# A chunked state-space scan feeding a squared-ReLU network: chunks of 64 tokens instead of 128, and every small product as a 32x32 tile

## The chip, the cores and the metric

The kernel runs on one core of a Trainium2 chip. The metric is the device time of one execution in microseconds (us), lower is better. The times of before are three runs on a chip; the profile is one more execution of the same program.

## What is computed

Inputs: x (4 batches, 8 heads, 768 tokens, 32 features), decays a (one per batch, head and token), B and C (16 states), and two matrices w_in (256 x 2048) and w_out (2048 x 256). Cut to what matters, the reference is:

```
for each chunk of tokens:                       # any chunk length gives the same y
    cum = cumsum(log a)                         # within the chunk
    M[i,j]   = (C_i . B_j) * exp(cum_i - cum_j)  for j <= i, else 0
    y        = M @ x  +  exp(cum_i) * (C_i @ state)
    state    = exp(cum_last) * state + sum_j exp(cum_last - cum_j) * B_j x_j
out = square(relu(y @ w_in)) @ w_out            # over 3072 tokens, the 8 heads' y side by side
```

The recurrence is per batch and head; the state is 16 x 32. The feed-forward part is most of the arithmetic.

## The kernel before, in words

**Units.** The 3072 tokens are cut into 12 units of 256 tokens (`UNITS`: three pieces j of a batch's 768 tokens, four batches b; units 0 to 3 are j=0, 4 to 7 j=1, 8 to 11 j=2). A token is 2p+r, with p the partition and r in 0, 1. Before, a unit has two chunks i of 128 tokens (64 partitions each).

**Scan of a unit k.** The decays become cumulative products P (`scan`, `prep_p`), C is multiplied by P (`prep_c`), x by 1/P (`prep_x`), B is copied as it is (`prep_b`). C and B of all heads stand side by side in a tile `jt`, which is transposed to `bct`: for units 0 to 3 by six products on TensorE (PE) and two copies (`ph_tr`, `ph_trc`), from unit 4 on by a DMA transpose. Then come the small products, all on PE:

- `ph_mt` (L213): scores C.B of the unit, 16 products of 32 x 64 weights on 256 columns, into all of banks 0 to 3. VectorE (DVE) multiplies them by the causal mask (`ph_mask`, L222, four of 512 elements) into `mts`.
- `ph_u` (L238): what each chunk adds to the state, 16 products of 64 x 32 on 64 columns (8 for j=2, whose last chunk has no successor).
- `ph_carry` (L238): C times the state before a chunk, 4 products of 128 x 128 on 128 columns (2 for j=0). Its weights `Sd` hold the state in a block-diagonal form that GpSimd (POOL) builds with `Pquad` (`ph_sd`, L329).
- `ph_intra` (L238): mts times x, 32 products of 64 x 32 on 128 columns, added in PSUM to the carry.
- `ph_t`, `ph_uc`: ScalarE (ACT) copies y to `T` and the state sums to `us`. `ph_z` (L313, L318, DVE) runs the recurrence over the chunks.

**Feed-forward.** For block k and each of eight groups: `mm1` (L388) is four products of 128 x 128 on 256 columns from T and w_in into one bank, ACT takes relu (L393), DVE squares (L399), `mm2` (L413) is four products of 128 x 128 on 256 columns into the block's accumulation bank. So there are 12 x 8 x 2 = 192 groups of four.

**Order.** All engines run their instructions in the order in which they are issued, and that order is the hand-written string `ORDER`: `c3` is `mm1` of block 2, group 3; `C3` its `mm2`; `mt1`, `mk1` (masks), `tr2`, `pc2`, `pb2`, `px2`, `ld3` (load of unit 3 on SP's queue) act on a unit; `rg6` is one region: carry of unit 5, u of unit 6, intra of unit 5, scores of unit 6, on PE one after the other. Units 1 and 2 are done in pieces (`eu`, `ey`, `et`) between the first groups. `bank()` hands out PSUM banks in turn from the list `turn` (4 and 5 first, then 4, 5, 0, 1, then 4, 5, 6) for mm1 and for y and u in `region`.

**Opening.** L439 on: loads of a, then C, B, x of units 0 and 1 on SP and ACT; a cumulative product; unit 0 up to T[0]; products of ones (`idle_products`, L458) fill PE while it has nothing to do, 21 in all. Weights come on POOL's queue, which converts them to bf16: w_in in two halves (groups 0 to 3, groups 4 to 7), w_out in four quarters. The first half is issued after a copy (`gate_w`) that waits for unit 0's B, the second after a copy (`gate_b`) that waits for unit 2's B; unit 3's load waits behind a POOL memset (`gate`).

Of the kernel before, what the change touches and what calls it, by code (L numbers as in the profile page):

```python
# [13 lines left out]
ALU = mybir.AluOpType  # L14
# [16 lines left out]
def kernel(  # L31
# [17 lines left out]
        a0 mt1 mk1 a1 sc1 a2 ld2 mk1 mk1 a3 A0 ms1 eu1 A1 sd1 A2 ey1 A3 iv0 la et1 b0 b1 b2 b3 w1 w2 px2 sn B0 ld3 pc2  # L49
        B1 w3 pb2 ld4 a4 tr2 B2 tc2 a5 b4 mt2 pc3 B3 mk2 p2 A4 mk2 b5 mk2 mk2 a6 eu2 pb4 sd2 pb3 B4 b6 A5 tr3 px3 tc3  # L50
        pc4 ey2 b7 a7 iv1 et2 B5 B6 A6 rg3 c0 px4 za3 sa3 ld5 tr4 mk3 mk3 c1 bk0 c2 zb3 A7 sb3 c3 mk3 pq pc5 px5 c4
        mk3 B7 ld6 c5 bk1 C0 c6 rg4 zb0 sb0 pb5 C1 mk4 C2 mk4 za4 c7 C3 tr5 ld7 zb1 zb4 sa4 sb4 pb6 d0 mk4 C4 C5 d1
        sb1 d2 mk4 C6 pc6 C7 d3 px6 d4 D0 rg5 tr6 mk5 za5 zb5 sa5 sb5 D1 iv2 mk5 d5 D2 pb7 d6 d7 D3 zb2 e0 mk5 e1 sb2
        D4 mk5 D5 ld8 pc7 e2 D6 e3 px7 D7 rg6 e4 za6 sa6 tr7 zb6 mk6 e5 sb6 e6 e7 mk6 E0 E1 E2 E3 ld9 px8 mk6 f0 E4 f1
        pc8 E5 pb8 E6 mk6 f2 f3 E7 rg7 mk7 F0 f4 za7 tr8 F1 F2 f5 f6 f7 g0 zb7 sa7 sb7 mk7 F3 mk7 F4 pc9 pb9 px9 ld10
        g1 F5 mk7 g2 F6 g3 F7 rg8 za8 zb8 sa8 sb8 g4 G0 mk8 tr9 g5 G1 mk8 g6 G2 g7 G3 mk8 h0 G4 pc10 pb10 px10 ld11 h1
        G5 mk8 h2 G6 h3 G7 rg9 za9 zb9 sa9 sb9 h4 H0 mk9 tr10 h5 H1 mk9 h6 H2 h7 H3 mk9 i0 H4 pc11 pb11 px11 i1 H5 mk9
        i2 H6 i3 H7 rg10 za10 zb10 sa10 sb10 i4 I0 mk10 tr11 i5 I1 mk10 i6 I2 i7 I3 mk10 j0 I4 j1 I5 mk10 j2 I6 j3 I7
        rg11 za11 zb11 sa11 sb11 j4 J0 mk11 j5 J1 mk11 j6 J2 j7 J3 mk11 k0 J4 k1 J5 mk11 k2 J6 k3 J7 rg12 k4 K0 k5 K1
        k6 K2 k7 K3 l0 K4 l1 K5 l2 K6 l3 K7 l4 L0 l5 L1 l6 L2 l7 L3"""  # L60
    WIN = [(0, 4), (4, 8)]
    WOUT = [(0, 2), (2, 4), (4, 6), (6, 8)]
# [8 lines left out]
    fpool = ctx.enter_context(tc.tile_pool(name="fpool", bufs=4))  # L71
    hpool = ctx.enter_context(tc.tile_pool(name="hpool", bufs=8))
# [3 lines left out]
    UNITS = [(b, j) for j in range(3) for b in range(4)]  # L76

    eye_f = const.tile([128, 128], FP32, name="eye_f")
    eye_b = const.tile([128, 128], BF16, name="eye_b")
    mask = const.tile([128, 512], BF16, name="mask")  # L80
    tri = const.tile([128, 2, 128], BF16, name="tri")
    warm = const.tile([128, 2], BF16, name="warm")
    quad = const.tile([128, 4], FP32, name="quad")
# [4 lines left out]
    a_nat = [const.tile([n, 128], FP32, name=f"a_nat{n}") for n in (64, 128)]  # L88
    a_cl = [const.tile([n, 128], FP32, name=f"a_cl{n}") for n in (64, 128)]
    cp = [const.tile([n, 128], FP32, name=f"cp{n}") for n in (64, 128)]  # L90
    pick_p = [const.tile([n, m], FP32, name=f"pick_p{n}") for n, m in ((64, 8), (128, 16))]
    P_sb = const.tile([128, 2, 96], FP32, name="P_sb")
    Pinv = const.tile([128, 2, 96], FP32, name="Pinv")
    Ptot = const.tile([128, 24], FP32, name="Ptot")
    Pquad = const.tile([128, 24, 4], FP32, name="Pquad")
    jt = [const.tile([128, 2, 3, 128], BF16, name=f"jt{i}") for i in range(3)]
    w_in_b = [wpool.tile([128, 2, (f1 - f0) * 256], BF16, name=f"w_in_b{i}") for i, (f0, f1) in enumerate(WIN)]
# [4 lines left out]
    def total(i, b, j):  # L102
        return 4 * i + b if j == 0 else 8 + 8 * i + 4 * (j - 1) + b

    def load_a(j, u, eng):
        row = 32 * u if j == 0 else 64 * u + 32 * (j - 1)
        t = a_nat[j > 0]
        eng.dma_start(out=t[row:row + 32, :], in_=_dap(a, j * 256 + u * 128, [[S, 32], [1, 128]]))
# [13 lines left out]
    def gate(k, what):  # L122
        b, j = UNITS[k]
        w = {"B": N, "C": N, "x": D}[what]
        t = nat.tile([128, NH, 2 * w], FP32, tag=f"{what}_nat", name=f"{what}_nat{k}")
        loaded.setdefault(k, {})[what] = t
        nc.gpsimd.memset(t[:, 0, 0:1], 0.0)

    def load_w_in(i):
        f0, f1 = WIN[i]  # L130
        n = (f1 - f0) * 256
        nc.gpsimd.dma_start(out=w_in_b[i], in_=_dap(moe_w_in, f0 * 256, [[2048, 128], [128 * 2048, 2], [1, n]]))

    def load_w_out(i):
        f0, _ = WOUT[i]
# [3 lines left out]
    def group_of(groups, fp):  # L139
        i = next(i for i, (f0, f1) in enumerate(groups) if f0 <= fp < f1)  # L140
        return i, fp - groups[i][0]

    live = {}

    def prep_c(k, eng, P=None):
        b, j = UNITS[k]
        for g in range(2):
            p = P_sb if P is None else P
            st = 96 if P is None else 32
            col = (j * 32 if P is None else 0) + b * 8 + 4 * g  # L150
            eng.tensor_tensor(  # L151
                out=_fap(jt[k % 3], 128 + 144 * g, [[384, 2], [32, 4], [1, 16]]),
                in0=_fap(loaded[k]["C"], 128 * g, [[16, 2], [32, 4], [1, 16]]),
                in1=_fap(p, col, [[st, 2], [1, 4], [0, 16]]), op=ALU.mult)

    def prep_b(k, eng, gs=(0, 1)):
        for g in gs:
            o = _fap(jt[k % 3], 16 * g, [[384, 2], [32, 4], [1, 16]])
            i = _fap(loaded[k]["B"], 128 * g, [[16, 2], [32, 4], [1, 16]])
            if eng is nc.scalar:  # L160
                eng.copy(out=o, in_=i)
            else:
                eng.tensor_copy(out=o, in_=i)  # L163

    def prep_x(k, eng):
# [8 lines left out]
        live.setdefault(k, {})["xs"] = xs  # L174

    def ph_tr(k, banks):

        v = live.setdefault(k, {})
        bct = big.tile([128, 2, 3, 128], BF16, tag="bct", name=f"bct{k}")
        v["bct"] = bct  # L180
        if banks is None:
            nc.sync.dma_start_transpose(out=bct.rearrange("p r w t -> p (r w) t"),
                                        in_=jt[k % 3].rearrange("p r w t -> p (r w t)"))
            return
        v["tr"] = []
        for r in range(2):
            h = banks[r]
            o = 0 if banks[0] != banks[1] else r * 192
            tr = pp[:, h, o:o + 192].bitcast(BF16)
            for w in range(3):  # L190
                nc.tensor.transpose(tr[:, w * 128:(w + 1) * 128], jt[k % 3][:, r, w, :], eye_b)  # L191
            v["tr"].append(tr)

    def ph_trc(k, engs):
        v = live[k]
        for r, eng in enumerate(engs):
            if eng is None:
                continue
# [6 lines left out]
    T = {}  # L205

    def ph_mt(k):
        v = live[k]
        bct = v["bct"]
        for r in range(2):  # L210
            for u in range(2):
                for q in range(4):
                    nc.tensor.matmul(  # L213
                        pp[64 * u:64 * u + 64, q, r * 256:r * 256 + 256],
                        bct[32 * q:32 * q + 32, r, 0, u * 64:u * 64 + 64],
                        _fap(bct[32 * q:32 * q + 32], 128 + u * 64, [[128, 2], [384, 2], [1, 64]]),
                        start=True, stop=True, skip_group_check=True,
                        tile_position=(32 * q, 64 * u))
        v["mts"] = big.tile([128, 4, 2, 2, 128], BF16, tag="mts", name=f"mts{k}")

    def ph_mask(k, q):
        nc.vector.tensor_tensor(out=live[k]["mts"][:, q].rearrange("p r g i -> p (r g i)"),  # L222
                                in0=pp[:, q, :], in1=mask, op=ALU.mult)

    def ph_score(k, q):
        sc = big.tile([128, 512], BF16, tag="sc", name=f"sc{k}_{q}")
        nc.scalar.copy(out=sc, in_=pp[:, q, :])  # L227
        live[k].setdefault("sc", {})[q] = sc

    def ph_mask_sb(k, q, eng):  # L230
        eng.tensor_tensor(out=live[k]["mts"][:, q].rearrange("p r g i -> p (r g i)"),  # L231
                          in0=live[k]["sc"][q], in1=mask, op=ALU.mult)

    def mm(begun, i, quads, dst, w, v, pos):
        need = [(i, q) for q in quads if (i, q) not in begun]
        begun.update(need)
        assert len(need) in (0, len(quads))
        nc.tensor.matmul(dst, w, v, start=bool(need), stop=False, skip_group_check=True,  # L238
                         **({} if pos is None else {"tile_position": pos}))

    def ph_carry(k, h, begun):
        for i in range(2):
            S_i = live[k]["S"][i]
            if S_i is None:
                continue
            for g in range(2):
                mm(begun, i, range(4), pp[:, h[i], g * 128:(g + 1) * 128], S_i[:, g * 128:(g + 1) * 128],
# [52 lines left out]
    def ph_z(k, i):  # L300
        b, j = UNITS[k]
        v = live[k]
        if j == 2 and i == 1:
            return
# [396 lines left out]
```

## Time and profile before

| what | us |
|---|---|
| median of three runs | 121.46 |
| the runs | 121.38, 121.46, 122.57 |
| profiled execution, first to last instruction (its span) | 119.2 |
| first mm1 starts | 12.5 |
| last mm2 product starts | 115.5 |
| PE busy from 40.35 to 102.85 | 62.50 of 62.50 |

The profile keeps no time of its own execution beyond the span: 121.46 - 119.2 = 2.3 us lie around it in the median run. Everything is read against that span. PE busy means that some product was in flight; the starts of neighbouring products tell how fast they go. From 40.35 us on PE never waits, until the last few products; the other engines have room there: DVE 51.49, ACT 44.13, POOL 27.57 of 62.50 us.

### The profile page before, as it was taken

The numbers are of one execution on the slowest core, as the hardware profiler recorded it, in microseconds if no ns is written. First come the engines' busy times: TensorE is split into PE (matmuls) and PEld (weight loads), VectorE is DVE, ScalarE is ACT, GpSimd is POOL, SyncE is SP. The second block draws the span as 40 slices with busy tenths as digits, with TensorE's granted clock in tenths as the row PEclk, the third lists the DMA queues.
The fourth block names the chain that finished last, engine by engine and source line by source line (L and its number), as shares of the span: only waits on it lengthen the run. The fifth ranks groups of instructions, "written<-read, shape, count | busy, mean of one in ns | idle before, by whom it ended". The sixth has DMA issues, their size and how long they took to land.

```text
span 119.2 us, 3961 instructions
## 1 busy us (share of the span) xinstructions
PE 111.2 (93%) x1609; PEld 93.1 (78%) x1609; DVE 83.0 (70%) x187; ACT 77.1 (65%) x158; POOL 49.3 (41%) x104
## 2 busy tenths in 40 slices
PE   7999879499989999999999999999999999999980
PEld 2533557278859898998998989989989889899960
DVE  5536593649489997999986798939848578445420
ACT  0735646475669667769565887686686777876840
POOL 7573387202676779565912297409120020000000
PEclk9999999999999999999999999999999999999999
DMA  2999968998991778998972854834023020020202
GB/s 41 198 157 162 219 139 97 185 178 162 192 144 59 188 149 149 198 135 178 74 150 93 139 108 138 145 105 105 3 89 70 0 96 0 0 93 0 88 0 88
DMA packets 47186, 13.46 MB, mean 113 GB/s; under 512 B 44288, under 2 KB 44736, under 8 KB 47168
## 3 DMA queue, kind: packets, MB, share of 16 engines
q1 hardware_dynamic: 44416, 10.83, 47.6%
q0 software_dynamic: 1120, 2.10, 11.0%
q10 hardware_dynamic: 1632, 0.28, 1.3%
q8 instruction: 12, 0.20, 0.7%
q14 instruction: 6, 0.05, 0.2%
HBM read 10.58 MB, written 3.15 MB: 115 GB/s over the span
## 4 chain that ended last, share of the span: by engine, by line
PE 83%; DMA 6%; ACT 3%; POOL 2%; DVE 1%; issue 1%; ACTq 0%; DVEq 0%
PE pp L388 33%; PE pp L413 32%; PE pp L238 6%; DMA w_in_b<-in_moe_w_in_dram 6%; PE pp L458 5%; PE pp L213 4%; ACT hb L393 2%; PE pp L191 1%; POOL mts L231 1%; PE pp L431 1%; POOL jt L151 1%; DVE mts L231 1%; PE pp L504 0%; ACT bct L201 0%; ACT sc L227 0%
## 5 line engine op out<-in xcount | busy, mean ns | idle before, releaser
L393 ACT ACTIVATE hb<-pp 128x512 bf16<-128x512 f32 x96 | 55.3, 599 | 25.5 <-PE pp L388 23.3
L388 PE MATMUL pp<-T,w_in_b 128*128 128x256 bf16 x384 | 54.8, 273 | 2.5 <-DMA w_in_b<-in_moe_w_in_dram 1.9
L399 DVE TENSOR_TENSOR h<-hb 128x512 bf16<-128x512 bf16 x96 | 45.2, 481 | 14.4 <-ACT hb L393 14.1
L413 PE MATMUL pp<-w_out_b,h 128*128 128x256 bf16 x384 | 54.9, 273 | 0.0
L388 PEld LDWEIGHTS <-w_in_b 128*128 128x128 bf16 x384 | 41.3, 114 | 6.0 <-DMA w_in_b<-in_moe_w_in_dram 2.3
L413 PEld LDWEIGHTS <-h 128*128 128x128 bf16 x384 | 36.7, 98 | 4.8 <-issue 0.8
L222 DVE TENSOR_TENSOR mts<-pp,mask 128x512 bf16<-128x512 f32 x44 | 29.4, 680 | 4.6 <-PE pp L213 4.6
L329 POOL TENSOR_TENSOR Sd<-z,Pquad 128x256 bf16<-128x256 f32 x16 | 10.7, 671 | 30.8 <-DVE z L313 24.3
L170 POOL TENSOR_TENSOR xs<-x_nat,Pinv 128x256 bf16<-128x256 f32 (+1 forms) x20 | 15.7, 798 | 3.3 <-DMA x_nat<-in_x_dram 1.8
L151 POOL TENSOR_TENSOR jt<-C_nat,P_sb 128x128 bf16<-128x128 f32 x22 | 9.7, 459 | 6.4 <-DMA C_nat<-in_C_dram 6.4
L458 PE MATMUL pp<-const-bfloat16-1.0 128*128 128x512 bf16 x13 | 6.2, 603 | 0.8 <-PEq L685 0.8
L420 ACT COPY osb<-pp 128x512 f32<-128x512 f32 x11 | 6.4, 586 | 0.2 <-PE pp L413 0.2
L313 DVE SCALAR_TENSOR_TENSOR z<-z,Ptot,us 128x64 f32<-128x64 f32 x8 | 2.2, 281 | 5.5 <-ACT us L297 5.4
L213 PE MATMUL pp<-bct 32*64 32x256 bf16 x192 | 5.3, 291 | 0.4 <-ACT us L294 0.3
L238 PE MATMUL pp<-mts,xs 64*32 64x128 bf16 x384 | 5.6, 219 | 0.0
L163 POOL CAST jt<-B_nat 128x128 bf16<-128x128 f32 x16 | 4.6, 317 | 1.9 <-DMA B_nat<-in_B_dram 1.9
L283 ACT CAST T<-pp 128x512 bf16<-128x512 f32 x8 | 4.7, 587 | 0.8 <-PE pp L238 0.5
L458 PEld LDWEIGHTS <-const-bfloat16-1.0 128*128 128x128 bf16 x21 | 2.1, 123 | 3.7 <-issue 3.4
L238 PE MATMUL pp<-bct,Sd 128*128 128x128 bf16 x40 | 4.2, 219 | 0.0
L238 PEld LDWEIGHTS <-xs 64*32 64x32 bf16 x384 | 3.8, 90 | 0.5
L238 PEld LDWEIGHTS <-jt 64*32 64x32 bf16 x160 | 1.6, 90 | 3.0 <-issue 1.0
L213 PEld LDWEIGHTS <-bct 32*64 32x64 bf16 x192 | 2.1, 105 | 2.1 <-issue 1.5
(71 smaller groups left out, 55.7 us busy)
## 6 DMA issues: line engine op xcount, KB each, us to landing
x_nat<-in_x_dram SPq DMA_DIRECT2D x11, 256.0 KB, 4.4
out_dram<-osb SPq DMA_DIRECT2D x11, 256.0 KB, 3.2
C_nat<-in_C_dram SPq DMA_DIRECT2D x11, 128.0 KB, 4.2
B_nat<-in_B_dram SPq DMA_DIRECT2D x11, 128.0 KB, 4.1
w_in_b<-in_moe_w_in_dram POOLq DMA_DIRECT2D x2, 512.0 KB, 7.1
w_out_b<-in_moe_w_out_dram POOLq DMA_DIRECT2D x4, 256.0 KB, 7.7
out_dram<-osl SPq DMA_DIRECT2D x2, 128.0 KB, 1.7
x_nat<-in_x_dram SPq DMA_DIRECT2D x1, 128.0 KB, 3.7
```

The source lines that it names most:

```text
L151: eng.tensor_tensor(out=_fap(jt[k % 3], 128 + 144 * g, [[384, 2], [32, 4], [1, 16]]), in0=_fap(loaded[k]["C"], 128 * g, [[16, 2], [32, 4], ...
L170: eng.tensor_tensor(out=_fap(xs, 256 * r, [[256, 2 // n], [32, 8], [1, 32]]), in0=_fap(loaded[k]["x"], 32 * r, [[32, 2 // n], [64, 8], [1, ...
L213: nc.tensor.matmul(pp[64 * u:64 * u + 64, q, r * 256:r * 256 + 256], bct[32 * q:32 * q + 32, r, 0, u * 64:u * 64 + 64], _fap(bct[32 * q:32 ...
L222: nc.vector.tensor_tensor(out=live[k]["mts"][:, q].rearrange("p r g i -> p (r g i)"), in0=pp[:, q, :], in1=mask, op=ALU.mult)
L238: nc.tensor.matmul(dst, w, v, start=bool(need), stop=False, skip_group_check=True, **({} if pos is None else {"tile_position": pos}))
L329: nc.gpsimd.tensor_tensor(out=_fap(S_d, 0, [[128, 2], [32, 4], [1, 32]]), in0=_fap(z, 0, [[32, 2], [0, 4], [1, 32]]), in1=_fap(Pquad, 4 * ...
L388: nc.tensor.matmul(pp[:, h, i * 256:(i + 1) * 256], _fap(w, g * w.shape[2] + (o // 2) * 512 + 2 * (o % 2) + i, [[4, 128]]), T[blk][:, g].r ...
L393: nc.scalar.activation(out=hb.rearrange("p i t -> p (i t)"), in_=pp[:, h, :], func=AF.Relu)
L399: nc.vector.tensor_tensor(out=h2, in0=hb, in1=hb, op=ALU.mult)
L413: nc.tensor.matmul(acc(blk, r), h2[:, i, r * 128:(r + 1) * 128], w_out_b[gi][:, 2 * o + i, :], start=first, stop=(fp == 7 and i == 1), ski ...
L420: nc.scalar.copy(out=osb, in_=pp[:, 6 if blk == 1 else 7, :])
L458: nc.tensor.matmul(pp[:, h, 0:cols], ones_b[:, 0:128], ones_b[:, 0:cols] if dep is None else dep, start=True, stop=True, skip_group_check= ...
```

## The change

- A unit has four chunks u of 64 tokens (32 partitions each), three of which have a successor at j=2.
- All small products are 32 x 32 tiles. Scores: 32 on 128 columns into columns 0 to 255 of banks 0 to 3. u: 32 on 64 columns (24 for j=2) into columns 384 to 447. Intra: 64 on 64 columns into columns 256 to 383 of the same banks. Carry: 32 on 64 columns (24 for j=0) into two banks of its own from `bank()`, one per half of the heads; the state needs no block-diagonal form any more (`Pquad` and `quad` go).
- Carry and intra no longer meet in PSUM: ACT copies the carry to `cs` and DVE adds the intra part into T (`ph_t`); for units 0 to 2 ACT copies intra (`ph_ys`) and DVE adds the carry (`ph_add`). The masks of a unit are two DVE instructions of 512 elements, not four; the recurrence is three or four z steps per unit, in place.
- Opening: a is loaded by one DMA per j on SP (128 rows of 64); scans run over 64 columns; prep_x of unit 0 moves from POOL to DVE; 15 products of ones remain, five of 128 columns and two of 256 among them. Unit 2 is loaded with unit 1.
- Weights come in eight pieces of two groups each, w_in and w_out in turn; the first is gated by unit 1's C. The gates of w_in's second half and of unit 3 go.
- `ORDER` is new: blocks a and b run their groups in twos, with banks 4 and 5 alone until block b ends, then 4, 5, 6. From `rg5` on the order is one region, then mm1 and mm2 alternating, as before.

The core of the diff; removed lines are left out.

```
+        a0 mA1 a1 u1 mB1 z1 sd1 A0 y1 A1 cy1 w6 pc2 b0 b1 w7 pb2 a2 B0 a3 B1 iv0 b2 b3 tr2 tc2 A2 mt2 A3 mA2 B2 mB2 px2
+        B3 la a4 a5 b4 b5 ld3 A4 u2 A5 z2 sd2 B4 B5 y2 a6 a7 sn sp cy2 b6 b7 pc3 pb3 px3 tr3 tc3 A6 A7 ld4 B6 c0 B7 c1
+        rg3 C0 c2 z3 sd3 iv1 pc4 pb4 C1 c3 mA3 px4 tr4 C2 c4 mB3 C3 c5 ld5 c6 pc5 pb5 px5 C4 c7 rg4 C5 z4 sd4 tr5 C6 mA4 d0 C7 d1 mB4 iv2 ld6 d2 pc6 pb6 px6 d3
+        rg5 d4 D0 z5 sd5 tr6 d5 D1 mA5 d6 D2 d7 mB5 D3 ld7 e0 D4 pc7 pb7 px7 e1 D5 e2 D6 e3 D7
...
+    PAIRS = [(0, 2), (2, 4), (4, 6), (6, 8)]
...
+    def load_a(j, eng):
+        eng.dma_start(out=a_nat[:, j, :], in_=_dap(a, j * 256, [[64, 4], [S, 32], [1, 64]]))
...
     def ph_mt(k):
...
         for r in range(2):
+            for u in range(4):
+                for R in range(4):
+                    p = slice(32 * R, 32 * R + 32)
                     nc.tensor.matmul(
+                        pp[32 * u:32 * u + 32, R, r * 128:r * 128 + 128],
+                        bct[p, r, 0, u * 32:u * 32 + 32],
+                        _fap(bct[p], 128 + u * 32, [[128, 2], [384, 2], [1, 32]]),
+                        start=True, stop=True, skip_group_check=True, tile_position=(32 * R, 32 * u))
...
+    def ph_carry(k, banks):
...
+        for s in range(4):
+            for R in range(4):
+                u = (R + s) % 4
+                if u == 0 and j == 0:
+                    continue
+                St = live[k - 4]["S"][:, 3] if u == 0 else live[k]["S"][:, u - 1]
+                p = slice(32 * R, 32 * R + 32)
+                for e in range(2):
+                    q = 2 * (R % 2) + e
+                    nc.tensor.matmul(pp[32 * q:32 * q + 32, banks[R // 2], u * 64:u * 64 + 64], St[p, e * 32:e * 32 + 32],
+                                     _fap(bct[p], 128 + 128 * e + 32 * u, [[384, 2], [1, 32]]), start=True, stop=True,
+                                     skip_group_check=True, tile_position=(32 * R, 32 * q))
...
+    def ph_u(k, base, begun):
...
+            for half in range(2):
+                for u in range(chunks(k)):
+                    p = slice(32 * u, 32 * u + 32)
+                    for R in ((0, 1), (2, 3))[(u + half) % 2]:
+                        mm(begun, u, R, pp[32 * R:32 * R + 32, base + u, U:U + 64],
+                           jt[k % 3][p, r, 0, 32 * R:32 * R + 32], v["xs"][p, r, 64 * R:64 * R + 64],
+                           (32 * u, 32 * R))
...
+    def ph_intra(k, base, begun):
         v = live[k]
         for g in range(2):
             for r in range(2):
+                for u in range(4):
+                    p = slice(32 * u, 32 * u + 32)
+                    for q in range(4):
+                        h = 4 * g + q
+                        mm(begun, u, q, pp[32 * q:32 * q + 32, base + u, Y + g * 64:Y + g * 64 + 64],
+                           v["xs"][p, r, 32 * h:32 * h + 32], v["mts"][p, h // 2, r, h % 2, :], (32 * u, 32 * q))
...
+    def region(y, u=None):
+
+        begun = set()
         h = sorted((bank(), bank()))
+        ph_carry(y, h)
         if u is not None:
+            ph_u(u, 0, begun)
+        ph_intra(y, 0, begun)
         if u is not None:
+            ph_mt(u)
+        ph_t(y, h)
+        if u is not None:
+            ph_us(u, 0)
...
+        gate = const.tile([128, 1], FP32, name="gate")
+        nc.gpsimd.tensor_copy(out=gate, in_=loaded[1]["C"][:, 0, 0:1])
+        load_w(0)
+        load_w(1)
+        idle_products(3, 5, 128, jt[0][:, 0, 0])
+        ph_mt(0)
...
+        ph_intra(0, 4, set())
+        ph_ys(0, 4)
+        ph_tr(1, (2, 3))
+        ph_carry(0, (0, 1))
+        ph_add(0, (0, 1))
         inv(8, 16)
...
+        load_w(3)
+        load_w(4)
+        load_w(5)
+        ph_mt(1)
...
         def second_p():
             h = bank()
+            for j in (1, 2):
+                prep_p(j, h, 64 * (j - 1))
...
+        def early_c(k):
+            h = sorted((bank(), bank()))
+            ph_carry(k, h)
+            ph_add(k, h)
```

In the new `ORDER`, `mA`, `mB` are the two masks of a unit, `u`, `y`, `cy` are u, intra and carry of units 1 and 2 (`early_c` above), `w6`, `w7` weight pieces, `la` the loads of a for j=1 and 2, `sn` and `sp` their scan and P (`second_p`); `rg3` is u and scores of unit 3 alone.

More of the change, by code (lines that the diff above doesn't have):

```diff
@@ L48 @@
     ORDER = """
[L49 to L53, printed above, removed]
@@ L219, in ph_mt @@
[L219 to L232, printed above, removed]
```

518 lines of the change are left out of this document (187 added, 331 removed).

## Prediction, made before the change was run

> **What bounds the kernel now.** I read the page's busy rows, then the chain that ended last in order of time, then the waits, then the timeline of PE alone around one region.
>
> ```profile
> span 119.2 us, 3961 instructions
> PE 111.2 (93%) x1609; PEld 93.1 (78%) x1609; DVE 83.0 (70%) x187; ACT 77.1 (65%) x158; POOL 49.3 (41%) x104
> ...
> PE   7999879499989999999999999999999999999980
> ```
>
> PE is the bound, except in the first third. The chain says the same: group after group of 0.44 us, and the region between them (238 and 213 are the small products).
>
> ```profile
> 46.13 0.44 PE pp L413 x4
> 46.57 0.73 PE pp L238 x52
> 47.30 0.35 PE pp L213 x16
> 47.65 0.54 PE pp L413 x4
> ```
>
> So every ns of small products in a region lengthens the kernel; masks and copies on DVE and ACT are hidden there. What a small product costs is seen in PE's timeline (start, us until the last of the group ends, what):
>
> ```profile
> 46.41 0.39 PE L238 MATMUL pp<-bct,Sd 128*128 128x128 bf16 x4
> 46.72 0.25 PE L238 MATMUL pp<-xs,jt 64*32 64x64 bf16 x16
> 46.79 0.51 PE L238 MATMUL pp<-mts,xs 64*32 64x128 bf16 x32
> 47.23 0.42 PE L213 MATMUL pp<-bct 32*64 32x256 bf16 x16
> 47.59 0.50 PE L413 MATMUL pp<-w_out_b,h 128*128 128x256 bf16 x3
> ```
>
> ```profile
> 103.00 0.42 PE L238 MATMUL pp<-mts,xs 64*32 64x128 bf16 x32
> ```
>
> The same 32 intra products take 0.51 us behind 16 others, and 0.42 us in the last region, where nothing small is ahead of them. Read one by one, the starts in the first region are: four carries 56 ns apart; the first u 149 ns after the last carry; 32 small products 3 to 4 ns apart in their bursts; 78 ns with none; the last 16 at 8.3 ns each, with their weight loads at the same 8.3 ns; then 155 ns to the first score (another tile shape); and 200 ns from the last score to the first big product. At j=2 (40 small ones) again exactly 32 are fast and the last 8 are 8.3 ns apart. So a store of 32 weight-and-product pairs goes fast, and is then refilled at 8.3 ns a pair; and each change of tile shape costs some 90 ns over the normal spacing.
>
> Of the first third, the waits and the timeline tell:
>
> ```profile
> PE pp L388 <- DMA w_in_b<-in_moe_w_in_dram: 1.9, 2, 1.6
> ```
>
> ```profile
> 0.84 2.72 PE L458 MATMUL pp<-const-bfloat16-1.0 128*128 128x512 bf16 x6 [0.84 <-PEq L685]
> 10.49 0.60 PE L458 MATMUL pp<-mts,const-bfloat16-1.0 128*128 128x512 bf16 x2
> 12.54 0.63 PE L388 MATMUL pp<-T,w_in_b 128*128 128x256 bf16 x4 [0.22 <-DMA w_in_b<-in_moe_w_in_dram]
> 18.92 1.94 PE L388 MATMUL pp<-T,w_in_b 128*128 128x256 bf16 x16
> 23.56 0.63 PE L388 MATMUL pp<-T,w_in_b 128*128 128x256 bf16 x4 [1.65 <-DMA w_in_b<-in_moe_w_in_dram]
> ```
>
> PE stands 1.65 us for w_in's second half. And products of 512 columns start 427 ns apart at first, 222 ns from 10.15 us on: half the clock until then, the full one after about 9 us of filled PE.
>
> **A. The regions, rg4 to rg12.** Before: 1.19 us from the first carry's start to the first big product (46.406 to 47.585), and 0.01 for its slower successor; 1.14 at j=2, 1.10 for rg4 and 0.69 for rg12 in the same way. After, one shape holds from carry to scores: 32 + 32 + 64 + 32 = 160 pairs. 0.09 for the change into the shape (149 - 56), 0.23 for the first 32 pairs and the gap (46.721 to 46.949), 128 x 8.3 ns = 1.06, then 0.15 out of it (200, less 53 as the last product streams 128 columns, not 256) and 0.03: 1.56 us. With 152 pairs (rg4, j=2) 1.49, with 96 (rg12) 1.03. The differences: 0.39 (rg4), 3 x 0.37, 4 x 0.35, 0.34: **+3.2 us**, all on PE's path. Bounds: if all pairs went at the fast 3.3 ns, a region would be 0.09 + 0.53 + 0.15 + 0.03 = 0.80, and the sum -3.2; the upper end is part E. I take 8.3 ns, which both kinds of region show from the 33rd pair on. The switch that goes away (some 0.09) is in this sum.
>
> The Trainium skill's page "TensorE: Matmul & The Clock Gate", in Part 3 (measured speedup against the span model), prices each further packed tile at about 4 ns. By that the sum would be near the lower end; the trace agrees for the first 32 pairs only.
>
> **B. Opening, to the first group of block b.** Before, b0 starts at 18.92 with 8 groups done. After, from rows: the scan as before; unit 0's two masks (0.69 and 0.42) instead of four, and one ACT copy of scores (0.59) instead of three; three z steps (0.28 each) and Sd (0.42) on DVE come newly ahead of the carry; so T[0] at about 10.9 (before 12.1), scores of unit 1 at 11.5, a0 at 11.9. Weights: unit 1's C is issued at 2.83 on SP and such loads land in 4.2 us (median of the DMA issues), so the first piece goes out at about 7, with half the bytes of before's, which took 7.5 us: it lands at about 11 to 12, just hidden. Then u1, masks, z1 (0.84), a POOL step (0.7), carry and ph_add (two DVE reads, 0.7) stand in a row before b0, because b0 needs T[1] and bank 4: b0 at about 17.0 with 4 groups done. Four more groups (1.75) against 1.92 us: -0.2, with two masks fewer **-0.3**. Bounds -1.5 (weights early, z1 hidden) to +1.5 (first piece late; POOL sits behind the gate, and prep_c of unit 1 behind two DMA issues of 0.6 to 0.8).
>
> **C. b0 to rg4.** Small products of units 2 and 3: intra 0.74 and carry 0.32 instead of 0.50 together, second_p with twice the products (some 1.1 for 0.72), u2 0.33 for 0.28, rg3 0.6 for 0.7: +0.9. The wait for w_in goes: -1.65; pieces 3 to 5 are issued on POOL behind prep_x of unit 1, at about 12 to 14, and land by 17 to 21, before their groups (21 to 25). PE's pauses between 31.8 and 34 (ACT's order around T[2]): -0.5. New waits: scores of unit 2 for the copies of its transposes, one group after them (0.7); four mm1 in a row on two banks, twice (relu takes 0.60 against 0.44 for a group: 0.4 to 0.5 each time); carry of unit 2 into banks 4 and 5, which wait for second_p's ACT copies (0.6), and b6 for the addition behind that (0.9). That is 3.1 if none is hidden; I take +2.0, bounds 0 and 4. **C = +0.75.**
>
> **D. The clock.** Before was full at 10.15, after a stretch with ones in every gap. After has fewer and shorter ones, and gaps near 7.3 to 8.4 and 10.1 to 11.4. If the full clock comes only after some microseconds of groups, each us of cold groups costs half of itself: 0 (as before) to 2.8 (cold until about 18). I take **+0.8**.
>
> **E. Refills of instructions.** Queue 8 brings PE's instructions (12 packets of 16 KB, 0.20 MB, for 3218 PE rows; 0.7% of 16 engines' span is 1.1 us a packet). After has about 1080 products more, so some 8 packets more; a region is 320 instructions in 1.3 us, more than one packet's 256, and one takes over 1 us. Before, a region of 136 never met that. 0 to 2.2 (a quarter of the regions wait 0.9 us each); I take **+0.3**.
>
> DVE and ACT add nothing: in a block of 8 us DVE has 8 squares (3.9), two masks (1.4), the sum into T (0.7) and four z steps (1.1), ACT 6.4. POOL loses half of Sd. Should PE get faster by 1 us a block, DVE would still fit.
>
> Sum: 3.2 - 0.3 + 0.75 + 0.8 + 0.3 = +4.75 on the profiled span of 119.2, which is 123.95; with the 2.27 that lie around it in the median run of 121.46: **126.2 us**.
>
> **Rivals.**
> 1. Faster: the store is refilled faster for 32 x 32 tiles, so all pairs go at 3.3 ns. For it: nothing in the trace says what sets 8.3 ns, and the tiles are half as large. Against: regions of j=1 and of j=2 both leave the fast pace at the 33rd pair, wherever that lies in the work. A = -3.2, the rest as above: 119.8. A region breaks even at (1.19 - 0.50) / 128 = 5.4 ns a pair. By the skill's 4 ns (the page named above) this rival wins.
> 2. The opening keeps all that its order offers: B = -1.5, no new waits in C, the clock as before: 126.2 - 1.2 - 2.0 - 0.8 = 122.2. For it: the 1.65 us wait does go. Against: two banks for all of blocks a and b, and relu slower than a group.
> 3. PE waits for its own instructions: E = 2.2, so 128.1. For it: twice the instructions per us in a region than anywhere before. Against: no wait of before is seen to be one. "Runtime: NRT & Kernel Launch" of the Trainium skill (Instruction fetch mechanics) gives PE room for 2048 instructions and calls the crossing mostly hidden; no run here shows that room, and by it this rival would be nil.
>
> **How the numbers follow.** Forecast 0.53; rival 1 0.25; rival 2 0.10; rival 3 0.12. Faster by over 1%, which is about what a measurement here can tell from none, means under 120.25, slower over 122.67. Rival 1 gives faster 0.15, same 0.07, slower 0.03 (B to D may spoil or help it); rival 2 0.02, 0.04, 0.04; the forecast and rival 3 slower, 0.65. So 0.17, 0.11, 0.72. The range reaches from rival 1's 119.8 to 130.0, the forecast with D or E near its upper end; a tenth is left out on each side. The forecast's own range is 123.5 to 129.
>
> **What would show it.** In a region after: some 32 fast pairs, then weight loads 8 ns apart, carry to first big product 1.5 to 1.6 us (A; under 1.0 is rival 1). b0 near 17, no wait for w_in_b at 20 to 25 us, waits of mm1 for ACT and DVE in blocks a and b (B, C). Groups of 0.87 us after 11 us (D). Gaps of about 1 us inside a region, named issue (E). I am wrong if PE's regions are shorter than before, or if the first third gains more than 3 us.

## The result, and the profile after

| what | before | after |
|---|---|---|
| median, us | 122.01 (four runs, 121.38 to 124.14) | 150.94 (148.88, 149.82, 152.05, 152.41) |
| ratio, 95% interval | | 1.228 [1.216, 1.240] |
| profiled execution: its time, its span | span 119.2 | 148.88, span 147.2 |

The change makes the kernel 23% slower; 4% was forecast, and 130.0 was the end of the range. Ratios, here and in the experiments, are of the faster runs of each kernel alone (of after 148.88 and 149.82; the other two are over 1.5% above the fastest). The page of the kernel after, its busy rows and its slices:

```profile
span 147.2 us, 6184 instructions
PE 122.4 (83%) x2715; PEld 101.0 (69%) x2715; DVE 81.9 (56%) x202; ACT 78.3 (53%) x154; POOL 41.5 (28%) x85
...
PE   7682969697349989475999999999599999999991
PEclk9955687999965999968799999999999999999999
```

PE has holes now until about 70 us and one at 105, and the granted clock drops to half five times before the end (at 7.21, 20.87, 41.35, 61.83 and 68.66 us). Before, there was neither from 40 us on. The region itself, in PE's timeline (start, us to the end of the last, what):

```profile
86.06 0.31 PE L231 MATMUL pp<-bct,S 32*32 32x64 bf16 x32
...
86.58 0.72 PE L216 MATMUL pp<-mts,xs 32*32 32x64 bf16 x64
...
87.54 0.63 PE L338 MATMUL pp<-T,w_in_b 128*128 128x256 bf16 x4
```

From the last big product before it to the fourth behind it, it takes 1.60 us more than big products alone would; before, 1.19 by the same reading. With 152 pairs it is 1.52, before 1.14. That is part A as forecast (1.56, 1.49). The rest is elsewhere. In the chain that ended last, in order of time (start, us, what), the longest times that PE is left are for a DMA and twice for "issue" (between them also for DVE, below):

```profile
7.79 6.48 DMA w_in_b<-in_moe_w_in_dram
...
65.23 2.66 issue
...
105.10 1.53 issue
```

I added up the starts of PE's products between the same numbers of finished groups of four. A product of 256 columns counts 0.109 us; what it takes more in a stretch at half clock is "half clock"; a gap over 0.25 us is "idle"; the rest is small products, ones and changes of tile shape.

| groups of the FFN done | before, us | after, us | more | idle | half clock | small and rest |
|---|---|---|---|---|---|---|
| 0 to 8 | 18.92 | 23.79 | +4.9 | +2.7 | +2.5 | -0.3 |
| 8 to 16 | 5.95 | 5.95 | 0 | -0.3 | +0.3 | 0 |
| 16 to 32 | 10.84 | 18.32 | +7.5 | +5.3 | +2.2 | 0 |
| 32 to 45 | 6.76 | 9.18 | +2.4 | +0.9 | +0.1 | +1.4 |
| 45 to 60 | 7.74 | 16.03 | +8.3 | +5.1 | +2.5 | +0.7 |
| 60 to 188 | 63.65 | 68.88 | +5.2 | +2.5 | 0 | +2.7 |
| 188 to the end | 5.3 | 5.0 | -0.3 | | | |

Of the 28.0 us, 16 are pauses of PE, 7.5 half clock, some 4.5 small products. What the pauses wait for, in the waits (us in total, times, longest):

```profile
PE pp L363 <- DVE h L349: 5.3, 5, 2.2
...
PE pp L192 <- issue: 2.7, 1, 2.7
```

The longest wait for DVE, in the timeline of all engines:

```profile
58.83 1.16 DVE L300 SCALAR_TENSOR_TENSOR z<-z,Ptot 128x64 f32<-128x64 f32 x3
...
59.90 0.68 DVE L200 TENSOR_TENSOR mts<-pp,mask 128x512 bf16<-128x512 f32 x1
60.50 1.18 DVE L349 TENSOR_TENSOR h<-hb 128x512 bf16<-128x512 bf16 x2
60.97 0.61 PE L363 MATMUL pp<-w_out_b,h 128*128 128x256 bf16 x4 [2.25 <-DVE h L349]
```

`C7` needs a square. On DVE it stands behind the sum into T (57.47 to 58.03), four z steps and a mask, all of them new or newly placed by the change (`C5 z4 sd4 tr5 C6 mA4 d0 C7`). DVE is 56% busy on the whole; the square still comes 2.25 us late. The same happens to B3 (pause of 1.12 at 28.16, from one start of PE's rows to the next) and to B5 (1.21 at 33.49).

The second kind of pause is inside a region, between two of its scores:

```profile
64.80 0.43 PE L192 MATMUL pp<-bct 32*32 32x128 bf16 x19
67.89 0.27 PE L192 MATMUL pp<-bct 32*32 32x128 bf16 x13 [2.66 <-issue]
```

No tile is late here. A packet of PE's instruction queue runs from 65.15 to 66.40 us, and PE goes on 1.5 us behind its end.

My theory after this reading: the pairs cost what was forecast; the loss is (1) pauses for work queued in the wrong order in blocks a to d, (2) instruction refills that a burst of 320 instructions outruns, (3) half clock that those pauses bring back. Rivals: the small products themselves cost more than their starts show; the fewer products of ones set the clock back; one late item (the squares, the first weights) is behind all pauses.

### The profile page after: what moved, and what is told of

It is laid out like the page before. It is cut to its first block, busy times and chain, and to the rows that moved or that the text cites. A ratio compares the mean times of both kernels' runs of the same rounds, so it can differ in the third digit from the quotient of the medians.

```text
span 147.2 us, 6184 instructions
## 1 busy us (share of the span) xinstructions
PE 122.4 (83%) x2715; PEld 101.0 (69%) x2715; DVE 81.9 (56%) x202; ACT 78.3 (53%) x154; POOL 41.5 (28%) x85
## 4 chain that ended last, share of the span: by engine, by line
PE 68%; DVE 8%; DMA 7%; issue 6%; ACT 6%; SPq 1%; POOL 1%; ACTq 0%; DVEq 0%; POOLq 0%
PE pp L338 31%; PE pp L363 27%; PE pp L216 5%; DMA w_in_b<-in_moe_w_in_dram 4%; DMA C_nat<-in_C_dram 3%; DVE z L300 3%; ACT hb L343 3%; PE pp L192 2%; DVE h L349 2%; PE pp L231 2%; DVE mts L200 1%; SPq L114 1%; POOL xs L156 1%; ACT z L293 1%; DVE T L286 1%
## 5 line engine op out<-in xcount | busy, mean ns | idle before, releaser
L338 PE MATMUL pp<-T,w_in_b 128*128 128x256 bf16 x384 | 61.5, 290 | 5.5 <-issue 2.0
L306 POOL TENSOR_TENSOR S<-z,Ptot 128x256 bf16<-128x256 f32 (+1 forms) x11 | 6.8, 616 | 50.7 <-DVE z L300 34.0
L200 DVE TENSOR_TENSOR mts<-pp,mask 128x512 bf16<-128x512 f32 x23 | 15.7, 684 | 2.3 <-PE pp L192 1.6
L274 DVE TENSOR_TENSOR T<-pp,cs 128x512 bf16<-128x512 f32 (+1 forms) x9 | 6.1, 677 | 16.8 <-PE pp L192 15.4
L300 DVE SCALAR_TENSOR_TENSOR z<-z,Ptot 128x64 f32<-128x64 f32 x32 | 9.6, 300 | 1.7 <-ACT z L293 0.7
L293 ACT COPY z<-pp 128x256 f32<-128x256 f32 (+1 forms) x12 | 4.3, 355 | 11.6 <-DVE T L274 11.4
L192 PE MATMUL pp<-bct 32*32 32x128 bf16 x384 | 6.1, 237 | 4.4 <-issue 2.7
L216 PE MATMUL pp<-mts,xs 32*32 32x64 bf16 x768 | 8.9, 201 | 0.2 <-DVE mts L200 0.2
L216 PEld LDWEIGHTS <-xs 32*32 32x32 bf16 x768 | 7.4, 89 | 1.4 <-issue 1.3
L271 ACT COPY cs<-pp 128x512 f32<-128x512 f32 (+1 forms) x9 | 5.3, 586 | 0.0
L216 PE MATMUL pp<-xs,jt 32*32 32x64 bf16 x352 | 4.9, 204 | 0.1
```

The costliest lines, as they stand in the source:

```text
L192: nc.tensor.matmul(pp[32 * u:32 * u + 32, R, r * 128:r * 128 + 128], bct[p, r, 0, u * 32:u * 32 + 32], _fap(bct[p], 128 + u * 32, [[128, 2 ...
L200: nc.vector.tensor_tensor(out=_fap(live[k]["mts"], h * 512, [[256, 2], [1, 256]]), in0=_fap(pp, h * 1024, [[512, 2], [1, 256]]), in1=_fap( ...
L216: nc.tensor.matmul(dst, w, v, start=first, stop=False, skip_group_check=True, tile_position=pos)
L300: nc.vector.scalar_tensor_tensor(out=z[:, i], in0=prev, scalar=c, in1=z[:, i], op0=ALU.mult, op1=ALU.add)
L306: eng.tensor_tensor(out=St[:, 0:n], in0=live[k]["z"][:, 0:n], in1=_fap(Ptot, j * 16 + b, [[4, n], [0, 64]]), op=ALU.mult)
L338: nc.tensor.matmul(pp[:, h, i * 256:(i + 1) * 256], _fap(w, g * 512 + 2 * o + i, [[4, 128]]), T[blk][:, g].rearrange("p r u t -> p (r u t) ...
```

## The experiments

All ratios are to the kernel before in the same series of runs; a kernel derived from after is compared with it by the ratios (after 1.228; 0.01 is 1.2 us).

**1. Before, each score and intra product cut into two column halves**: a region of 116 small products instead of 68, and nothing else changed.

```
-                for q in range(4):
-                    nc.tensor.matmul(pp[..., r * 256:r * 256 + 256], ..., [[128, 2], [384, 2], [1, 64]]))
+                for g in range(2):
+                    for q in range(4):
+                        nc.tensor.matmul(pp[..., r * 256 + g * 128:r * 256 + g * 128 + 128], ..., [[384, 2], [1, 64]]))
```

> Before with every score product (256 columns) and every intra product (128 columns) cut in two halves of columns: the same work and the same tiles, but 80 pairs of u and intra instead of 48, 32 score pairs instead of 16. If the number of pairs is what made the regions longer: a region goes from 1.19 to about 1.5 us, weight loads 8.3 ns apart from the 33rd pair on, and the kernel takes 3 to 4 us more, up to 6.5 if instruction refills stall PE too. If the 32 x 32 shape or the carry's own banks made them longer, and not the number: within 1 us of before.

Measured 125.55, ratio 1.034 [1.025, 1.043]: 4.0 us more. In PE's timeline the halved region:

```profile
49.20 0.90 PE L239 MATMUL pp<-mts,xs 64*32 64x64 bf16 x64
50.03 0.44 PE L214 MATMUL pp<-bct 32*64 32x128 bf16 x32
```

The same columns in more pairs: intra takes 0.90 instead of 0.51 us, and the region 1.60 instead of 1.19; the later regions take 1.40 to 1.46. It is the number of pairs that costs, not the columns. By the adding up above, small products are 3.0 us of it from group 16 on, and another 1.3 us are a window at half clock (25.37 to 28.78 us) that before does not have. So the some 3 us of part A are real, and they cannot be more than a seventh of the loss.

**2. Before, with the fifteen products of ones of after** (counts and columns as there, in before's places).

```
-        idle_products(4, 5, 128, jt[0][:, 0, 1:2]...)
+        idle_products(2, 5, 128, jt[0][:, 0, 1:2]...)
...
-        idle_products(1, 5, 256, live[0]["S"][1])
```

> Before with the 15 products of ones of after, at the same kinds of places, instead of 21. If the ones decide when the clock is granted: the full clock comes after 13 us instead of 10.15, the first groups start 218 ns apart instead of 109, and the kernel takes 1.5 to 3.5 us more. If the groups of block a bring the clock by themselves soon enough: 0 to 0.8 us more.

Measured 121.34, ratio 1.004 [1.001, 1.006]. PE's timeline:

```profile
14.02 2.75 PE L388 MATMUL pp<-T,w_in_b 128*128 128x256 bf16 x12
...
24.01 0.63 PE L388 MATMUL pp<-T,w_in_b 128*128 128x256 bf16 x4 [0.72 <-DMA w_in_b<-in_moe_w_in_dram]
```

The half clock does come back (12 products in 2.75 us), from 8.5 to 18.7 us, and slows the first eight groups by 2.5 us. The wait for w_in's second half at 24 us shrinks from 1.65 to 0.72, idle time elsewhere goes too, and 0.4 us of the loss are left (group 16 is done at 25.32 instead of 24.87): the weights were what this stretch waited for. Fewer ones by themselves are not the cause.

**3. Before, with w_in in four pieces of two groups**, the second issued ahead of w_out's first quarters, the third where the second half was, the fourth at `w2`.

```
-    WIN = [(0, 4), (4, 8)]
+    WIN = [(0, 2), (2, 4), (4, 6), (6, 8)]
...
+        load_w_in(1)
         load_w_out(0)
```

> Before with w_in in four pieces of two groups, the third issued where the second half was, the fourth behind it. If w_in's second half cost before its 1.65 us: 1.0 to 1.6 us faster. If that wait only stood in for ACT's order behind it (the pauses near 32 to 34 us): 0 to 0.5 faster; the additional DMA issues on POOL could cost as much.

Measured 119.89, ratio 0.989 [0.982, 0.996]: 1% faster than before. PE's timeline:

```profile
13.86 1.07 PE L388 MATMUL pp<-T,w_in_b 128*128 128x256 bf16 x8 [1.08 <-DMA w_in_b<-in_moe_w_in_dram]
...
15.69 0.68 PE L413 MATMUL pp<-w_out_b,h 128*128 128x256 bf16 x4 [0.76 <-DMA w_out_b<-in_moe_w_out_dram]
```

a0 starts at 10.77 (before 12.54) and the wait at 23.6 is gone; these two waits take most of it back, and group 16 is done at 23.83 instead of 24.87. So the smaller pieces, one part of the change, are worth about 1 us by themselves in the kernel before; in after nothing of it is left at group 8 (23.79 against 18.92).

**4. After, each square directly behind its relu** on DVE.

```
                 mm1(blk, fp)
-                if before:
-                    square(*before)
-                before = (blk, fp)
+                square(blk, fp)
```

> After with each square issued on DVE right behind its relu, ahead of the masks, z steps and additions that stand before it now. If PE's pauses in blocks a to d are squares that queue behind other DVE work: the wait of 2.25 us near 58 us and those near 18, 28 and 33 us shrink, some half-clock windows go with them, and the kernel takes 3 to 7 us less than after. If the pauses only change their name (masks and z late instead): within 1.5 us of after.

Measured 151.41, ratio 1.255 [1.245, 1.265]: no gain, rather a loss. The wait of `C7` is gone, and in the timeline the next region's carry stands instead:

```profile
61.68 1.02 POOL L138 TENSOR_TENSOR jt<-C_nat,P_sb 128x128 bf16<-128x128 f32 x2 [4.80 <-DMA C_nat<-in_C_dram]
...
65.20 0.31 PE L231 MATMUL pp<-bct,S 32*32 32x64 bf16 x30 [2.77 <-POOL S L306]
```

With the squares first, unit 3's z steps start at 52.57 instead of 50.32, behind a square that itself waits for its relu. The queues of POOL and SP hand the delay on: unit 5's C is issued at 57.14 instead of 54.89, POOL waits 4.80 us for it, and unit 4's S, which stands behind it on POOL, starts only at 64.35, though the last z step that it needs ended at 61.51. The wait has only changed its name; "the squares queue behind too much" falls as the single cause. It is not DVE's work alone that is late: the queues of DVE, POOL and SP wait for each other in turn.

**5. After, a region in two places**: carry and intra, and two group pairs later u and scores (token `um`).

```
-        rg5 d4 D0 z5 sd5 tr6 d5 D1 mA5 d6 D2 d7 mB5 D3
+        rg5 d4 D0 tr6 d5 D1 um5 z5 sd5 d6 D2 mA5 d7 D3 mB5
```

> After with each region from rg4 on in two places: carry and intra (96 pairs) first, u and scores (64 pairs) behind the second pair of groups that follows. If PE's waits named issue near 65, 80 and 105 us are instructions that come too late for a burst of 320: these waits (2.9, 0.7, 1.8 us) and the half clock near 70 us go, and the second change of tile shape costs 0.24 us in each of 8 regions: 3 to 5 us less than after in all. If those waits are for data or banks: they stay, and the kernel takes about 2 us more than after.

Measured 144.98, ratio 1.188 [1.180, 1.196]: some 5 us less than after, the upper end of the first expectation. What is left of the stall in PE's timeline:

```profile
68.89 0.33 PE L192 MATMUL pp<-bct 32*32 32x128 bf16 x29 [0.73 <-issue]
```

Groups 45 to 60 take 12.2 us instead of 16.0: 2.2 less idle, and the 2.5 us of half clock in them are gone too.

**6. After, with 64 products of ones of one column in the opening**: 128 more instructions of PE, half of a 16 KB packet, ahead of everything.

```
+        idle_products(64, 5, 1)
         prep_x(1, nc.gpsimd)
```

> After with 64 one-column products of ones (128 PE rows) more in the opening, where PE waits anyway. If the issue waits are page boundaries of the instruction stream: they come at the same row numbers as in after (2241, 2753, 4033, or others that differ from these by multiples of 256), so 128 rows earlier in the work, and in other regions. If they belong to the work: at the same places of the work, 128 row numbers later. The time may move either way by up to 4 us.

One run, 150.94; span 149.1. The stalls in PE's timeline:

```profile
61.14 0.28 PE L192 MATMUL pp<-bct 32*32 32x128 bf16 x17 [1.55 <-issue]
...
87.65 0.27 PE L192 MATMUL pp<-bct 32*32 32x128 bf16 x13 [1.35 <-issue]
```

They stand at other places of the work. Counted in PE's rows of the trace (weight loads, products and a handful of its sequencer's), the stalls of after come at rows 2241, 2753 and 4033, those here at 449, 1985, 3265, 4545 and 5057: all of them 193 above a multiple of 256. The place is fixed in the stream of instructions, in steps of one packet (16 KB, so 256 rows of 64 bytes), not in the work. The traces of experiments 4, 7 and 8 have long stalls at 2241, 2753 and 4033 too.

**7. After, another order at the end of block b**: the preparation of unit 3 ahead of B4, the relus between a6 and b7 spread, second_p later.

```
- A4 u2 A5 z2 sd2 B4 B5 y2 a6 a7 sn sp cy2 b6 b7 pc3 pb3 px3 tr3 tc3 A6 A7 ld4 B6 c0 B7 c1
+ A4 u2 A5 z2 sd2 pc3 pb3 B4 B5 a6 a7 y2 A6 px3 cy2 A7 tr3 tc3 b6 b7 sn ld4 B6 c0 B7 sp c1
```

> After with the end of block b ordered anew: unit 3's preparation before it, intra and carry of unit 2 behind a6 and a7 with A6 between them, scan and P of j=1, 2 behind b7 and B7. If PE's pauses of 4.6 us between 36.6 and 48.2 us come from that order, and the half clock of 2.2 us there from the pauses: 4 to 7 us less than after. If they only move on to the next wait: within 1.5 us of after.

Measured 147.59, ratio 1.210 [1.202, 1.218]: some 2 us less than after, between the two expectations. Groups 16 to 32 take 13.8 us instead of 18.3: 2.2 us of half clock go, 1.3 of idle, and part of second_p's products moves on. In the profiled run 3.2 of these 4.5 us come back elsewhere, 1.6 of them by a window at half clock from 104.17 us. The later pauses are untouched: C7 still waits 2.07 us for its square, and in PE's timeline stands

```profile
64.49 0.32 PE L192 MATMUL pp<-bct 32*32 32x128 bf16 x12 [2.78 <-issue]
```

This is the stall at row 2241 again, 3.5 us earlier and behind work in another order. At rows 2753 and 4033 PE stands too (0.68 and 1.75 us from start to start), where the profile names z of DVE.

**8. After, the first weights gated by unit 0's B** instead of unit 1's C.

```
-        nc.gpsimd.tensor_copy(out=gate, in_=loaded[1]["C"][:, 0, 0:1])
+        nc.gpsimd.tensor_copy(out=gate, in_=loaded[0]["B"][:, 0, 0:1])
```

> After with the first weights behind unit 0's B instead of unit 1's C. If a0's start at 14.3 is the late issue of its weights: a0 starts 1 to 2 us earlier and the kernel gains 1 to 2 us. If the weights then take the DMA engines from unit 1's x and unit 2: a0 earlier, but the next waits grow by as much, within 1 us of after.

Measured 151.91, ratio 1.233 [1.225, 1.242]: no gain; a0 does not start earlier (14.84). PE's timeline:

```profile
14.61 0.30 PE L192 MATMUL pp<-bct 32*32 32x128 bf16 x6 [2.07 <-issue]
```

With the weights earlier, refills are late in the scores of unit 1 (row 449), and again in its carry (1.55 at 21.90). Whether the transfer of the weights delays them is not settled; the late weights were not the only thing ahead of a0.

**9. After with the edits of 5 and 7 together.**

> The kernel after with both edits that helped alone: the region in two places (alone 144.98, 6.0 us less than 150.94) and the new order at the end of block b (alone 147.59, 3.3 us less). If the two took away causes of their own (instruction refills inside a burst; work queued in the wrong order in blocks a and b), they add up: 141.7, with groups 16 to 32 near 13.8 us and groups 45 to 60 near 12.2. If the waits only change their names, as when the squares were moved, the larger edit alone is left: 145.

Measured 142.75, ratio 1.164 [1.154, 1.175]: 0.064 less than after, some 8 us, where the two alone (0.040 and 0.018) add up to 0.058. Groups 16 to 32 take 13.8 us, groups 45 to 60 take 13.1. PE's timeline:

```profile
57.92 0.61 PE L362 MATMUL pp<-w_out_b,h 128*128 128x256 bf16 x4 [1.67 <-DVE h L348]
...
65.09 0.33 PE L192 MATMUL pp<-bct 32*32 32x128 bf16 x29 [1.01 <-issue]
```

The two edits take away causes of their own. Half clock is left only in the opening (up to 25.9 us, by the spacing of the products; the clock's own rows begin there); both pauses near 60 us are shorter, and no half clock follows them. What still lies between this and before, 21.5 us of span, is 11.4 idle, 4.0 half clock and some 6 of small products and changes of tile, by the same adding up.

**10. Before, with three pauses** late in the work, where it had none: in blocks j, k and l a product of ones waits for two POOL products behind a relu.

```
+            nc.gpsimd.tensor_tensor(out=s1, in0=hb, in1=hb, op=ALU.mult)
+            nc.gpsimd.tensor_tensor(out=s2, in0=s1, in1=s1, op=ALU.mult)
...
+            idle_products(1, 3, 128, s2[...][:, 0:128])
```

> The kernel before with three pauses of PE late in the work, where it had none: in blocks j, k and l one product of ones waits for two POOL products of 512 elements behind a relu. Each pause is 0.6 (relu) + 2 x 1.1 (POOL) + some 0.2 less one group of 0.44: 2.6 us, 7.7 in all. If the half clock belongs to the opening alone, the time is that of before plus the pauses: 121.5 + 7.7 = 129.2, and all groups behind the pauses start 0.44 us apart. If a pause anywhere brings it back (my reading of the kernel after, where each stretch at half clock is 3.4 us or two of them and follows pauses), each pause is followed by about 3.4 us with groups of 0.87, which costs 1.7 more: 134.3.

Measured 133.34, ratio 1.089 [1.082, 1.097]. The windows, cut where the granted clock may change (stretch, us, busy us of PE, PEld, DVE, ACT, POOL with their instructions, clock, DMA share, GB/s):

```profile
93.61:97.03 3.42, 0.70 (x8) 0.51 (x6) 0.55 (x2) 0.48 (x1) 2.32 (x2) 1.00 0.00 0
97.03:100.44 3.41, 3.41 (x70) 2.15 (x68) 0.29 (x2) 1.95 (x5) 0.00 (x0) 0.50 0.22 76
...
107.27:110.68 3.41, 1.56 (x45) 1.32 (x44) 0.24 (x1) 0.87 (x2) 1.72 (x2) 1.00 0.00 0
110.68:114.09 3.41, 3.41 (x47) 3.21 (x32) 1.32 (x4) 2.58 (x6) 0.00 (x0) 1.00 0.23 82
```

All three pauses are 2.72 us long. The first leaves PE busy for 0.70 us of one window, and the next window is granted half the clock. The third does the same (1.18 us busy from 114.09, half clock from 117.51 to 120.92). The second pause, from 106.4 to 109.1, is cut by the edge of a window, leaves 2.54 and 1.56 us, and the clock stays.

**11. The same pauses, filled** with ten products of ones of 512 columns each.

```
+            idle_products(10, 3)
             idle_products(1, 3, 128, s2[...][:, 0:128])
```

> The same three pauses with ten products of ones of 512 columns (2.1 us at the full clock) ahead of the product that waits. Both theories: PE goes on as late as with the pauses, but the clock stays: 121.5 + 7.7 = 129.2 and no group of 0.87 us. The difference to the run with empty pauses is what the half clock costs: 5 us by the theory that pauses bring it back, 0 by the other.

Measured 130.95, ratio 1.062 [1.053, 1.070]: 0.027 less than with empty pauses, some 3.3 us, though PE has more to do. PE's timeline:

```profile
93.94 2.35 PE L458 MATMUL pp<-const-bfloat16-1.0 128*128 128x512 bf16 x10
...
96.88 0.60 PE L388 MATMUL pp<-T,w_in_b 128*128 128x256 bf16 x4
```

No group behind a pause is slow. A pause costs its own length, and by chance of the windows' edges a window at half clock on top: in the profiled run two windows cost 2.1 us by the adding up above, and the runs differ by 3.3 us where 5 was expected for three. A size was missed, too: the pauses with what waits cost 2.9 us each, not 2.6.

**12. Before, with the second piece of w_in directly behind the first**, else as 3.

```
         load_w_in(0)
+        load_w_in(1)
```

> The kernel before with w_in in four pieces (119.89), the second piece now issued directly behind the first. If the wait of a2 (1.35 us at 12.5) came from the late issue, it goes and the time is 118.5. If the two transfers only share the DMA engines, the first lands later by what the second gains, and the time stays at 119.9.

Measured 119.98, ratio 0.980 [0.974, 0.985]: 2% faster than before. Whether it is faster than 3 is open (0.989, with intervals that overlap; the profiled spans are 118.4 and 118.2 us). Neither expectation holds as written. PE's timeline:

```profile
32.89 0.25 PE L238 MATMUL pp<-xs,jt 64*32 64x64 bf16 x16 [0.93 <-POOL xs L170]
```

a0 is even earlier (10.53), the wait for the second piece is halved (0.54 at 13.08), and group 16 is done at 22.66, 1.2 us ahead of 3. At 32.89 PE waits for x of a unit, which POOL has not got ready, and at group 32 the lead is gone (34.91 against 34.67 for the start of the same mm1). POOL itself waits for a C (6.06 us, to 27.75) and a B (2.38 us, to 31.07), so the next bound of the first third is the loads and POOL's work behind them.

## Why the prediction was right and wrong

The sum gave +4.75 us of span, and +28.0 were measured: 16 of pauses, 7.5 of half clock, some 4.5 of small products. A was nearly right; the sentence that put DVE and ACT at nothing failed, and the terms B, C, D and E were too small.

**Right: the direction, and part A.** The 33rd and every later pair of an unbroken run costs the 8.3 ns forecast: a region takes 1.60 and 1.52 us (forecast 1.56 and 1.49), and experiment 1 shows it alone: 48 pairs more in a region, and the kernel is 4.0 us slower, 3.0 of it small products. In rg4 a pause of 0.34 us is followed by some 30 fast pairs again. Rival 1 (3.3 ns for all pairs, a faster kernel) is dead. The Trainium skill's page "TensorE: Matmul & The Clock Gate", in Part 3, prices a further packed tile at about 4 ns; the runs agree only up to the 32nd pair, and that holds for 32 x 32 tiles as for larger ones. Rival 2 is dead as well: the wait for w_in at 20 to 25 us did go, and more came. Several waits that C named are there nearly as sized (from start to start): scores of unit 2 for their copies (0.54, forecast 0.7), two banks for four mm1 (0.52, forecast 0.4 to 0.5), b6 for the addition (0.92, forecast 0.9).

**Wrong: the sentence "DVE and ACT add nothing".** It summed a block of 8 us and found room, and a sum over a block says nothing of due times. The pauses that C did not name are of this kind: B3 and B5 for a square (1.12, 1.21), second_p for the scan (1.46), the transposes of unit 3 for ACT behind the relu of b7 (1.76), C7 (2.51 with the wait above). C's "+2.0, bounds 0 and 4" for new waits was a list of the waits that I could think of; groups 16 to 60 alone have 11.3 us more idle time, 2.7 of it a refill. Experiments 4 and 7 give the cause its form: in-order queues in which several things fall due at once. Moving one of them ahead only makes the next one late (4, no gain); another order of the whole stretch gains some 2 us (7).

**Wrong: E, a size and a mechanism that was half seen.** I had the numbers (a region of 320 instructions in 1.3 us, packets of 256, over 1 us a packet), and then took +0.3, because no wait of before was seen to be one. The refills cost pauses of 2.93, 0.73 and 1.80 us in the profiled run of after, about 5.2 net of the usual spacing, above the upper bound of 2.2: a missed refill costs up to 2.9 us, not 0.9. Experiment 6 shows that they sit at the packets' edges, experiment 5 that shorter bursts take most of them away. Rival 3 was the right mechanism, with too small a price. The page "Runtime: NRT & Kernel Launch" of the Trainium skill (Instruction fetch mechanics) calls the crossing mostly hidden and gives PE room for 2048 instructions; a wait of 2.66 us within a burst of 320 does not agree with "hidden" here. In the 14 traces no packet started with more than 286 rows of PE left before the edge that it serves (how edges and packets belong together stands under "Not settled"), so here about one packet is fetched ahead.

**Wrong: D, "0 to 2.8".** The forecast saw the clock as a matter of the opening. The half clock costs 7.5 us in the FFN's products, 4.7 of them from group 16 on, in windows that follow pauses. Experiment 2 shows that the fewer ones alone cost 0.4 us; 10 and 11 show the mechanism alone: empty pauses bring the half clock back, filled ones do not, for some 3.3 us. The Trainium skill's page "TensorE: Matmul & The Clock Gate" (Part 1) has the clock fall after an idle window of about 3.4 us and rise after a busy one; the runs agree with the window's length, and show that it need not be idle: 0.70 and 1.18 us of work in it did not keep the clock. So the parts of the sum were not independent: each pause of C and E could be priced again by D.

**Wrong: B, -0.3.** b0 starts at 20.47, not 17.0, with four groups done. The first piece of w_in lands at 14.27 (forecast 11 to 12): it is issued at 7.79 (forecast 7) and takes 6.48 us, where the forecast left 4 to 5 for half the bytes of a load of 7.5; 1.2 us are half clock. Another 0.66 is the scan's later start, at 3.45 us instead of 2.79, behind a's one DMA instead of two: "the scan as before" was wrong. Experiment 8 shows that the gate by itself is not what holds a0.

**Not settled.** The nine regions of after have some 2670 rows and so some 10 edges of packets, and only three stalls are long. The traces show which: counted in order, packet n fits the edge at row 256n + 193, and in none of 223 edges does PE pass earlier than 1.24 us behind the end of its packet; in the 24 stalls of over 0.4 us it goes on 1.24 to 1.62 us behind it. After's three stalls are at the edges whose packets started with 0, 28 and 34 rows left (at 65.15, 78.86 and 104.30 us). A refill is late, then, because its packet starts late for the pace of the rows behind it; what sets that start stays open. Experiment 8's stalls in the opening suggest that other transfers delay a refill; no run took that apart. The spread of after's runs (148.88 to 152.41) is not explained: their clocks on record (0.907 in the fastest, 0.921 in the slowest) do not follow the times. And of the 28.0 us, edits took away some 8 (experiment 9); the other pauses, in the opening above all, are read from one trace and no edit removed them.

## What to carry to other kernels

Before replacing few large products by many small ones, count pairs, not columns, and count the instructions of the longest burst (here 320) against a packet of 256; split a burst that comes near it. Cost a reordering by what is queued ahead of each item that PE needs, engine by engine at the moment it is due, not by the room in an average block, and price each pause of PE again for the clock that it may take away. When a large rewrite holds one good part (here the smaller pieces of w_in, 1 to 2% faster in experiments 3 and 12), try that part alone on the old kernel.

## What the runs showed of the hardware that was not expected

- A refill of PE's instructions can stop it for 0.7 to 2.9 us, each time at rows that are 193 above a multiple of 256 of its stream (after, and experiment 6), behind or inside a run of small products; the kernel before, with 12 packets, shows none.
- The clock is granted for windows of 3.41 us, whose edges do not follow the program's work (7.21 us in after, 8.60 in experiment 7, whose opening is the same). In after, too, the window ahead of a slow one is a thin one:

```profile
58.42:61.83 3.41, 1.17 (x11) 0.87 (x10) 3.25 (x8) 0.82 (x3) 1.73 (x4) 1.00 0.52 92
61.83:65.24 3.41, 3.40 (x157) 2.40 (x156) 1.77 (x4) 2.61 (x5) 0.91 (x2) 0.50 0.67 146
```

  PE busy for 1.17 us of a window is followed by half clock, and so is 0.78 us from 65.24 to 68.66. Near the middle it is open: 1.56 us in experiment 10 was not, 1.59 us of mostly small products in after (37.94 to 41.35) and 2.06 us in experiment 6 (84.75 to 88.16) were.
- A stretch at half clock costs little while PE waits for weights anyway (experiment 2: 2.5 us of it, the time 0.4% longer).
